# Sliding-window attention with a gated MLP: q and k transposes in PSUM banks of their own, evictions and loads in another order

## The chip, the cores and the metric

One core of a Trainium2 chip. The time is device microseconds of one execution of the program, as a median over runs; lower is better.

## What is computed

```python
# attention, per batch (8) and head (8): 576 positions, head size 64
scores = q @ k.T / sqrt(64)
mask   = (0 <= i - j) & (i - j < 64)          # the last 64 positions
attn   = softmax(where(mask, scores, -1e9))
x      = attn @ v                              # heads side by side: (8, 576, 512)
# gated MLP, per batch
h      = relu(x @ w_in)                        # (576, 1024)
u, v   = h[..., :512], h[..., 512:]
v_n    = (v - mean(v)) / sqrt(var(v) + 1e-6)   # over the last axis
v_s    = einsum('ts,bsd->btd', w_spatial, v_n) + b_spatial[None, :, None]
out    = (u * v_s) @ w_out                     # (8, 576, 512), float32
```

## The kernel before

The kernel works batch by batch. While the MLP of batch a runs, the attention of batch a+1 is worked in between its pieces, and q, k and v of later batches are loaded. Each engine executes its instructions in the order in which the program writes them; that order is written by hand, as strings of two-letter pieces that `run(a, ...)` reads.

The attention of a batch has five steps s: four for the head pairs 0 to 3 over 512 positions, and a fifth for the last 64 positions of all heads. A step goes through these pieces:

- `T` (batches 0 to 3 only): TensorE transposes k and q of the pair into one PSUM tile `tp` (`T_mm`), and `T_out` copies them to `tr` in SBUF, k on VectorE (DVE, L180) and q on ScalarE (ACT, L183). For batches 4 to 7 DVE does this itself, without TensorE, in two halves of two instructions each (`turn`, L147; letters T, or R one batch further ahead).
- `A`: the scores `sc` (`emit_S`), the exponential on ACT and the minimum with a mask on DVE (`E_exp`, `E_mask`), then for the step before it the products with v and the row sums (`emit_P`, tile `oz`), their logarithm and the exponential of its negative on ACT (`ln`, `zi`), and the product `x` on DVE (`N_mul`). The `x` product is written behind the next MLP piece; F writes it at once.

The MLP of a batch goes through V (five row blocks of v: matmul, ReLU on ACT, statistics `st` and `mv` on DVE; p are parts of the matmul and o the eviction; Q is the fifth block, which shares its PSUM tile with the last output block of the batch before and writes that block's store), L (layer norm: two small ACT operations, five DVE operations `vn`, L514), U (five column blocks of u with a ReLU on ACT), W (in batch 0 only, the transposes of w_spatial and their copies), G (the product with w_spatial, and on DVE the product `g` with u) and O (the output blocks, copied on ACT and stored by SP's queue, L476).

PSUM has two banks for `sc`, two for `oz`, and four for everything else, which are handed out in turn (tag "mm"). SP's queue issues the loads of q, k, v and the stores in program order, and waits in that order. POOL casts and shifts the loaded data (`batch_in`, L177). The tiles of loaded data have two buffers, those of cast q and k have one.

The prologue runs the attention of batch 0 pair by pair, with matmuls on zeros (`warm`) in between, and then half of the V matmuls of batch 0 ahead of its P of step 3.

## Time and profile before

| | |
|---|---|
| median of 3 runs | 246.35 us (244.47 to 248.13) |
| profiled execution | 246.02 us, span 244.3 us |
| PE, DVE, ACT, POOL busy, share of the span | 85%, 65%, 64%, 48% |
| prologue, up to the first U matmul of batch 0 (30.06) | 30.06 us |
| batch 0, up to the first transpose for batch 1's stage (63.93) | 33.87 us |
| batch 1, up to batch 2's first V matmul (93.75) | 29.82 us |
| batches 2, 3 (from V to V) | 30.11, 27.21 us |
| batches 4, 5, 6 | 24.25, 24.26, 23.12 us |
| batch 7, to the end | 21.60 us |

The stages are cut by hand at the starts of instructions. A row of a timeline gives the start, the time, the engine, the line of the kernel, the operation and its operands, how many such instructions are put together, and in brackets how long the engine stood idle before it and what ended that. "PE" is TensorE. A share of busy time is an average over stages with different limits, so the table is read by stage.

### The profile page before, as it was taken

The numbers are of one execution on the slowest core, as the hardware profiler recorded it, in microseconds if no ns is written. First come the engines' busy times: TensorE is split into PE (matmuls) and PEld (weight loads), VectorE is DVE, ScalarE is ACT, GpSimd is POOL, SyncE is SP. The second block draws the span as 40 slices with busy tenths as digits, with TensorE's granted clock in tenths as the row PEclk, the third lists the DMA queues.
The fourth block names the chain that finished last, engine by engine and source line by source line (L and its number), as shares of the span: only waits on it lengthen the run. The fifth ranks groups of instructions, "written<-read, shape, count | busy, mean of one in ns | idle before, by whom it ended". The sixth has DMA issues, their size and how long they took to land.

```text
span 244.3 us, 6707 instructions
## 1 busy us (share of the span) xinstructions
PE 207.1 (85%) x2727; PEld 112.1 (46%) x2727; DVE 157.8 (65%) x312; ACT 156.4 (64%) x284; POOL 118.0 (48%) x162
## 2 busy tenths in 40 slices
PE   7577896876976778966999699989998999999993
PEld 2345344553443444534544454545454545554451
DVE  6554379735544753676767677897789778774650
ACT  2365585476476665678578547884788578957713
POOL 3999648999104992227700794992099100000000
PEclk9995999999997999999999799999999999999999
DMA  6999999995009956999999999599960032004105
GB/s 188 300 194 267 217 281 184 275 204 181 4 9 269 262 92 209 196 196 212 200 194 268 244 201 201 180 201 195 180 212 10 3 128 66 6 3 173 24 0 193
DMA packets 77647, 40.43 MB, mean 165 GB/s; under 512 B 44272, under 2 KB 73008, under 8 KB 77616
## 3 DMA queue, kind: packets, MB, share of 16 engines
q1 hardware_dynamic: 75392, 37.76, 70.0%
q0 software_dynamic: 2224, 2.24, 5.4%
q8 instruction: 21, 0.34, 0.7%
q14 instruction: 10, 0.08, 0.2%
HBM read 32.79 MB, written 9.44 MB: 173 GB/s over the span
## 4 chain that ended last, share of the span: by engine, by line
PE 47%; DVE 26%; ACT 20%; issue 5%; POOL 0%; ACTq 0%; POOLq 0%
PE ps L544 11%; PE po L563 11%; PE pv L457 9%; DVE vn L514 6%; ACT e L359 6%; DVE x L429 5%; DVE st L466 4%; DVE tr L180 4%; ACT tr L183 4%; PE oz L394 3%; ACT zi L421 3%; DVE e L375 3%; PE oz L404 2%; ACT vs L464 2%; PE pv L491 2%
## 5 line engine op out<-in xcount | busy, mean ns | idle before, releaser
L177 POOL COPY vs<-vn 64x512 f16<-64x512 f16 (+1 forms) x56 | 44.9, 802 | 3.1
L375 DVE TENSOR_TENSOR e<-e,mask 128x1024 f16<-128x1024 f16 x32 | 27.1, 846 | 28.3 <-ACT e L359 28.3
L177 POOL CAST nk<-fk 128x512 f16<-128x512 f32 (+2 forms) x24 | 20.3, 846 | 51.2 <-DVE tr L147 25.1
L544 PE MATMUL ps<-wspT,vn 128*128 128x512 f16 (+1 forms) x160 | 40.1, 394 | 5.5 <-ACT tr L183 2.3
L429 DVE TENSOR_TENSOR x<-oz,zi 128x512 f16<-128x512 f32 (+1 forms) x40 | 25.3, 633 | 25.7 <-ACT zi L421 25.0
L359 ACT ACTIVATE e<-sc 128x1024 f16<-128x1024 f32 x32 | 32.9, 1028 | 11.1 <-PE sc L317 7.1
L457 PE MATMUL pv<-win,x 128*128 128x512 f16 (+1 forms) x132 | 32.2, 384 | 1.1 <-DVE x L429 1.1
L177 POOL CAST vn<-vf 128x512 f16<-128x512 f32 (+1 forms) x40 | 27.3, 692 | 9.2 <-DMA vf<-in_v_dram 8.5
L466 DVE BATCH_NORM_STATS2 st<-vs 128x6 f32<-128x512 f16 (+1 forms) x40 | 27.0, 675 | 7.3 <-ACT vs L464 6.9
L524 PE MATMUL pu<-x,win 128*128 128x512 f16 x128 | 30.4, 380 | 0.0
L563 PE MATMUL po<-wout,g 128*128 128x512 f16 x128 | 30.2, 379 | 0.0
L464 ACT ACTIVATE vs<-pv 128x512 f16<-128x512 f32 (+1 forms) x40 | 23.0, 596 | 9.0 <-PE pv L457 7.0
L183 ACT COPY tr<-tp 128x512 f16<-128x512 f16 x16 | 9.4, 586 | 29.2 <-DVE tr L180 29.2
L566 ACT COPY ob<-po 128x512 f32<-128x512 f32 x32 | 18.7, 586 | 12.0 <-PE po L563 12.0
L177 POOL CAST nq<-fq 128x512 f16<-128x512 f32 (+2 forms) x27 | 22.3, 825 | 8.3 <-DMA fq<-in_q_dram 8.1
L547 DVE TENSOR_TENSOR g<-ps,ru 128x512 f16<-128x512 f32 x32 | 21.9, 686 | 6.2 <-PE ps L544 6.0
L412 ACT ACTIVATE ln<-oz 128x512 f32<-128x512 f32 (+1 forms) x40 | 22.3, 559 | 5.6 <-PE oz L404 5.6
L544 PEld LDWEIGHTS <-vn 128*128 128x128 f16 (+1 forms) x160 | 14.8, 100 | 23.1 <-issue 5.7
L421 ACT ACTIVATE zi<-ln 128x512 f32<-128x512 f32 (+1 forms) x40 | 23.7, 592 | 0.8
L514 DVE TENSOR_SCALAR vn<-vs,mv,rs 128x512 f16<-128x512 f16 (+1 forms) x40 | 19.8, 560 | 1.2 <-ACT rs L506 1.2
L394 PE MATMUL oz<-e,onesK 128*64 128x512 f16 x64 | 13.4, 410 | 6.8 <-DVE x L429 6.6
L457 PEld LDWEIGHTS <-x 128*128 128x128 f16 (+1 forms) x132 | 12.1, 99 | 15.3 <-DVE x L429 1.6
(81 smaller groups left out, 298.8 us busy)
## 6 DMA issues: line engine op xcount, KB each, us to landing
out_dram<-ob SPq DMA_DIRECT2D x32, 256.0 KB, 3.5
vf<-in_v_dram SPq DMA_DIRECT2D x40, 128.0 KB, 5.1
fk<-in_k_dram SPq DMA_DIRECT2D x32, 144.0 KB, 4.8
fq<-in_q_dram SPq DMA_DIRECT2D x32, 144.0 KB, 5.8
fk<-in_k_dram SPq DMA_DIRECT2D x16, 256.0 KB, 4.9
fq<-in_q_dram SPq DMA_DIRECT2D x16, 256.0 KB, 5.2
vf<-in_v_dram SPq DMA_DIRECT2D x16, 256.0 KB, 6.6
win<-in_moe_w_in_dram POOLq DMA_DIRECT2D x2, 512.0 KB, 8.4
```

The costliest lines, as they stand in the source:

```text
L177: nc.gpsimd.tensor_copy(o, i)
L359: nc.scalar.activation(e2[:, :, :], sc[0][:, :, :], AF.Exp, bias=0.0, scale=0.125)
L375: nc.vector.tensor_tensor(e2[:, :, :], e2[:, :, :], m, ALU.min)
L421: nc.scalar.activation(zinv[:, 0:n], lnz[:, 0:n], AF.Exp, bias=0.0, scale=-1.0)
L429: nc.vector.tensor_tensor(x[:, 0:n], oz[:, 0, 0:n], zinv[:, 0:n], ALU.mult)
L457: nc.tensor.matmul(PV[b, j][0:jn, :], xcol(b, r, j), w_in_sb[:, r, 512:1024], start=(r == 0), stop=(r == 3))
L464: nc.scalar.activation(vs[0:jn, :], pv[0:jn, :], AF.Relu)
L466: nc.vector.bn_stats(st6[0:jn, 0:6], vs[0:jn, :])
L514: nc.vector.tensor_scalar(vn[0:jn, :], vs[0:jn, :], mv[0:jn, j, 0:1], rs[0:jn, j:j + 1], ALU.subtract, ALU.mult)
L524: nc.tensor.matmul(pu[:, :], w_in_sb[:, r, 128 * m:128 * m + 128], X[b, r][:, :], start=(r == 0), stop=(r == 3))
L544: nc.tensor.matmul(ps[:, :], VN[b, kk][0:kn, 128 * m:128 * m + 128], wspT[kk][0:kn, 0:512], start=(kk == 0), stop=(kk == 4))
L563: nc.tensor.matmul(po[:, :], G[b, r][:, 128 * j:128 * j + 128], w_out_sb[:, r, :], start=(r == 0), stop=(r == 3))
```

## The change

The change has these parts:

1. `T_mm` gives k and q a PSUM tile each (two of the four "mm" banks instead of one), and `T_out` copies the fifth step's q on ACT and no longer on DVE.
2. In the prologue `T_out` stands ahead of `N_mul`; the masks are made with fewer, larger copies, and `maskr`, `mv` and `vn4` are filled behind the first `T_out`; there are 3 warming matmuls where 4 were, and 4 more ahead of P of step 3; three quarters of V stand behind that P.
3. For batches 0 and 1 the ReLU of the V blocks 1 and 3 is done by DVE.
4. The strings of batches 0 to 3 are written anew: the attention of the next batch starts earlier (Y is the first transpose of the batch after next), statistics and norm stand behind the evictions of the transposes, and batch 3 has the string of the batches after it.
5. Batch 3's load is issued at the end of batch 0's string, ahead of the store of batch 0's last block, and no longer behind that store in Q of batch 1. The loads of batches 5 to 7 (a+3) move from Q of batch a to the end of batch a's string, ahead of the next store of a last block. Batch 4's load stays at the end of batch 1's string.

```diff
--- before.py
+++ after.py
@@ -213,22 +213,25 @@
                             base=64, channel_multiplier=-1, pattern=[[1, 64]])
     mask = cpool.tile([128, 2, 8, 64], f16, name="mask")
     maskr = cpool.tile([128, 8, 64], f16, name="maskr")
-    for u in range(8):
-        if u % 2 == 1:
-            nc.vector.tensor_copy(mask[:, 0, u, :], keep[:])
-        else:
-            nc.vector.tensor_scalar(mask[:, 0, u, :], keep[:], -1.0, BIG, ALU.mult, ALU.add)
-    nc.vector.memset(mask[64:128, 0, 0, :], 0.0)
+    nc.vector.tensor_scalar(mask[:, 0, 0, :], keep[:], -1.0, BIG, ALU.mult, ALU.add)
+    nc.vector.tensor_copy(mask[:, 0, 1, :], keep[:])
+    nc.vector.tensor_copy(mask[:, 0, 2:4, :], mask[:, 0, 0:2, :])
+    nc.vector.tensor_copy(mask[:, 0, 4:8, :], mask[:, 0, 0:4, :])
     nc.vector.tensor_copy(mask[:, 1, :, :], mask[:, 0, :, :])
-    for u in range(8):
-        nc.vector.tensor_copy(maskr[:, u, :], mask[:, 0, 2, :])
+    for h in (0, 1):
+        nc.vector.memset(mask[64:128, h, 0, :], 0.0)
 
     NSB = 2
     mv_t = [cpool.tile([128, 5, 2], f32, name=f"mv{i}") for i in range(NSB)]
     vn4_t = [cpool.tile([65, 512], f16, name=f"vn4_{i}") for i in range(NSB)]
-    for i in range(NSB):
-        nc.vector.memset(mv_t[i][:], 1.0)
-        nc.vector.memset(vn4_t[i][64:65, :], 1.0)
+
+    def late_consts():
+        nc.vector.tensor_copy(maskr[:, 0, :], mask[:, 0, 2, :])
+        for n in (1, 2, 4):
+            nc.vector.tensor_copy(maskr[:, n:2 * n, :], maskr[:, 0:n, :])
+        for i in range(NSB):
+            nc.vector.memset(mv_t[i][:], 1.0)
+            nc.vector.memset(vn4_t[i][64:65, :], 1.0)
 
     w_in_sb = cpool.tile([128, 4, 1024], f16, name="win")
     w_out_sb = cpool.tile([128, 4, 512], f16, name="wout")
@@ -256,31 +259,28 @@
     TP = {}
 
     def T_mm(b, s):
-        tp = psp.tile([128, 1024], f16, tag="mm", bufs=4, name=f"tp{b}_{s}")
+        tp = [psp.tile([128, 512], f16, tag="mm", bufs=4, name=f"tp{b}_{s}{x}") for x in "kq"]
         TP[b, s] = tp
-        n = 512 if s < 4 else 256
         with nc.named_scope(f"T{b}_{s}"):
             for y, x in enumerate("kq"):
                 w = NH[b, x, s]
                 for t in range(4):
                     if s < 4:
-                        nc.tensor.transpose(tp[:, n * y + 128 * t:n * y + 128 * t + 128],
+                        nc.tensor.transpose(tp[y][:, 128 * t:128 * t + 128],
                                             w[:, 128 * t:128 * t + 128], id16[:, :])
                     else:
-                        nc.tensor.transpose(tp[:, n * y + 64 * t:n * y + 64 * t + 64],
+                        nc.tensor.transpose(tp[y][:, 64 * t:64 * t + 64],
                                             w[0:64, 128 * t:128 * t + 128], id16[0:64, 0:64])
 
     def T_out(b, s):
         tp = TP.pop((b, s))
         o = TR[b][:, :, :].rearrange("p x (a n) -> p x a n", a=4)
-        for y in (0, 1):
+        for y, copy in ((0, dve_copy), (1, act_copy)):
             if s < 4:
-                (act_copy if y == 1 else dve_copy)(
-                    o[:, y, s, 0:512].rearrange("p (n t) -> p n t", t=4),
-                    tp[:, 512 * y:512 * y + 512].rearrange("p (t n) -> p n t", t=4))
+                copy(o[:, y, s, 0:512].rearrange("p (n t) -> p n t", t=4),
+                     tp[y][:, :].rearrange("p (t n) -> p n t", t=4))
             else:
-                nc.vector.tensor_copy(o[:, y, :, 512:576],
-                                      tp[:, 256 * y:256 * y + 256].rearrange("p (a n) -> p a n", a=4))
+                copy(o[:, y, :, 512:576], tp[y][:, 0:256].rearrange("p (a n) -> p a n", a=4))
 
     def emit_T(b, s):
         T_mm(b, s)
@@ -461,7 +461,10 @@
         jn = 128 if j < 4 else 64
         pv = PV.pop((b, j))
         vs = mpool.tile([128, 512], f16, tag=f"vs{j}", bufs=1, name=f"vs{b}_{j}")
-        nc.scalar.activation(vs[0:jn, :], pv[0:jn, :], AF.Relu)
+        if b < 2 and j % 2 == 1:
+            nc.vector.tensor_scalar_max(vs[0:jn, :], pv[0:jn, :], 0.0)
+        else:
+            nc.scalar.activation(vs[0:jn, :], pv[0:jn, :], AF.Relu)
         st6 = mpool.tile([128, 8], f32, tag="st6", bufs=6, name=f"st6{b}_{j}")
         nc.vector.bn_stats(st6[0:jn, 0:6], vs[0:jn, :])
         nc.vector.bn_aggr(mv_t[b % NSB][0:jn, j, :], st6[0:jn, 0:6])
@@ -601,6 +604,8 @@
             if c == "A":
                 if a + 1 < B:
                     att(a + 1, n)
+            elif c == "Y":
+                emit_T(a + 2, n)
             elif c == "T":
                 if a + 1 < NPE:
                     emit_T(a + 1, n)
@@ -622,12 +627,6 @@
             else:
                 if c == "Q":
                     emit_VO4(a)
-                    if a == 1:
-                        load_any(3)
-                        batch_in(3)
-                    elif 1 < a and a + 3 < B:
-                        load_any(a + 3)
-                        batch_in(a + 3)
                 elif c == "L":
                     emit_LN(a)
                 elif c == "W":
@@ -683,9 +682,11 @@
             warm(2)
         if s > 0:
             E_mask(0, s - 1)
+        T_out(0, s)
         if s > 1:
             N_mul(0, s - 2)
-        T_out(0, s)
+        if s == 0:
+            late_consts()
         emit_S(0, s)
         E_exp(0, s)
         if s == 3:
@@ -695,47 +696,48 @@
             emit_N1(0, s - 1)
             N_exp(0, s - 1)
         if s < 3:
-            warm(4)
-    T_out(0, 4)
-    E_mask(0, 3)
-    N_mul(0, 2)
+            warm(3)
     v_in(0, 4)
     load_wsp()
     load_wout()
     load_pairs(2)
     batch_in(1)
 
+    T_out(0, 4)
+    E_mask(0, 3)
+    N_mul(0, 2)
     emit_S(0, 4)
     E_exp(0, 4)
-    run(0, "p0002 p0102 p0202 p0302")
+    warm(4)
     emit_P(0, 3)
     emit_N1(0, 3)
     emit_N2(0, 3)
     E_mask(0, 4)
-    run(0, "p0023 p0123 p0223 p0323 p0034 o0 p0134 o1")
+    run(0, "p0003 p0103 p0203 p0303")
     emit_P(0, 4)
+    run(0, "p0034 p0134 p0234 p0334 o0 o1 o2 o3")
     emit_N1(0, 4)
     emit_N2(0, 4)
-    run(0, "p0234 o2 p0334 o3")
-    run(0, "U0 U1 T0 U2 Q A0 F U3 L W0 W1 W2 W3 W4 U4 T1 G0 A1 G1 G2 T2 G3 A2 G4")
+    run(0, "U0 U1 T0 U2 Q A0 F U3 T1 L A1 U4 W0 W1 W2 W3 W4 G0 G1 T2 A2 G2 G3 G4")
     batch_in(2)
-    run(0, "O0 O1 T3 A3 O2 O3 T4 F A4 F p1002 p1102")
-    run(0, "A5 p1202 p1302 p1023 p1123 p1223 p1323 F")
+    run(0, "O0 T3 A3 O1 O2 T4 F A4 F O3")
+    load_any(3)
+    run(0, "Y0 p1002 p1102 A5 p1202 p1302 p1023 p1123 p1223 p1323 F")
 
     for a in range(1, B):
         if a == 1:
-            run(a, "p0034 o0 p0134 o1 p0234 o2 p0334 o3 T0 U0 T1 U1 A0 Q L T2 U2 U3 A1 U4 G0 T3 A2 "
-                   "G1 G2 A3 T4 G3 G4 A4 O0 O1 A5 O2 O3")
-            load_any(4)
-            batch_in(4)
+            run(a, "A0 p0034 p0134 p0234 p0334 o0 o1 o2 o3 U0 T1 U1 A1 Q T2 F L U2 A2 U3 U4 T3 "
+                   "G0 A3 G1 G2 T4 G3 A4 G4 O0 O1 A5 O2 O3")
         elif a == 2:
-            run(a, "V0 T0 V1 T1 A0 V2 V3 Q T2 A1 F L U0 U1 U2 T3 A2 U3 U4 G0 T4 A3 G1 G2 G3 A4 "
-                   "G4 O0 O1 A5 O2 O3")
-        elif a == 3:
-            run(a, "T0 V0 V1 A0 V2 V3 Q A1 F L T1 U0 U1 U2 U3 A2 U4 G0 A3 G1 G2 G3 A4 G4 R0 O0 O1 "
-                   "A5 O2 R1 O3")
+            run(a, "V0 T0 V1 A0 V2 T1 V3 Q A1 T2 F L U0 U1 U2 A2 T3 U3 U4 G0 A3 T4 G1 G2 G3 A4 "
+                   "G4 R0 O0 O1 A5 O2 R1 O3")
         else:
             run(a, "V0 V1 A0 V2 V3 Q A1 F L U0 U1 U2 A2 U3 U4 G0 A3 G1 G2 G3 A4 G4 R0 O0 O1 A5 O2 R1 O3")
+        if a == 1:
+            batch_in(3)
+        if a + 3 < B:
+            load_any(a + 3)
+            batch_in(a + 3)
     run(B, "Q")
 
 
```

What this does to the order on three engines, at the places in question. In the names, the digits are step or block numbers; `tr`, `e`, `x`, `vn`, `wspT`, `g` are the tiles named above.

First DVE, in batch 0's MLP, from the mask of batch 1's first step to G. Before:

```order
L375 TENSOR_TENSOR e2_1_0_734<-e2_1_0_734,mask_175 128x1024
L514 TENSOR_SCALAR vn0_0_749<-vs0_0_625,mv0_195,rs0_746 128x512
L514 TENSOR_SCALAR vn0_1_751<-vs0_1_632,mv0_195,rs0_746 128x512
L514 TENSOR_SCALAR vn0_2_753<-vs0_2_657,mv0_195,rs0_746 128x512
L514 TENSOR_SCALAR vn0_3_755<-vs0_3_664,mv0_195,rs0_746 128x512
L514 TENSOR_SCALAR vn4_0_197<-vs0_4_711,mv0_195,rs0_746 64x512
L180 COPY wspT3_209<-wps3_779 128x576
L180 COPY wspT4_210<-wps4_786 64x576
L180 COPY tr1_123<-tp1_1_813 128x512
L547 TENSOR_TENSOR g0_0_832<-ps0_0_825,ru0_0_670 128x512
L375 TENSOR_TENSOR e2_1_1_852<-e2_1_1_852,mask_175 128x1024
L547 TENSOR_TENSOR g0_1_884<-ps0_1_877,ru0_1_678 128x512
```

and now:

```order
L375 TENSOR_TENSOR e2_1_0_732<-e2_1_0_732,mask_175 128x1024
L180 COPY tr1_123<-tp1_1k_743 128x512
L517 TENSOR_SCALAR vn0_0_760<-vs0_0_640,mv0_184,rs0_757 128x512
L517 TENSOR_SCALAR vn0_1_762<-vs0_1_645,mv0_184,rs0_757 128x512
L517 TENSOR_SCALAR vn0_2_764<-vs0_2_650,mv0_184,rs0_757 128x512
L517 TENSOR_SCALAR vn0_3_766<-vs0_3_655,mv0_184,rs0_757 128x512
L517 TENSOR_SCALAR vn4_0_186<-vs0_4_709,mv0_184,rs0_757 64x512
L375 TENSOR_TENSOR e2_1_1_787<-e2_1_1_787,mask_175 128x1024
L429 TENSOR_TENSOR x1_0_834<-oz1_0_790,zi1_0_832 128x512
L180 COPY wspT3_194<-wps3_857 128x576
L180 COPY wspT4_195<-wps4_864 64x576
L550 TENSOR_TENSOR g0_0_878<-ps0_0_871,ru0_0_667 128x512
```

The k copy of step 1 has moved ahead of the five norm operations, and the mask of step 1 and the x product of step 0 ahead of the copies of w_spatial, behind which G waits.

Then SP's queue, from the second store of batch 0's output to batch 3's first loads. Before:

```order
L476 DMA out_0_dram<-ob0_1_1030 128x512
L476 DMA out_0_dram<-ob0_2_1094 128x512
L476 DMA out_0_dram<-ob0_3_1107 128x512
L476 DMA out_0_dram<-ob0_4_1315 64x512
L83 DMA fk3_1318<-in_k_dram 128x2x256
L83 DMA fq3_1324<-in_q_dram 128x2x256
L122 DMA vf3_1331<-in_v_dram 128x4x64 x2
```

and now:

```order
L479 DMA out_0_dram<-ob0_1_1086 128x512
L479 DMA out_0_dram<-ob0_2_1099 128x512
L479 DMA out_0_dram<-ob0_3_1168 128x512
L83 DMA fk3_1171<-in_k_dram 128x2x256
L83 DMA fq3_1177<-in_q_dram 128x2x256
L122 DMA vf3_1184<-in_v_dram 128x4x64 x2
L83 DMA fk3_1171<-in_k_dram 128x2x256
```

The store of the last block (64x512), which waits for the next batch's Q, now stands behind all of batch 3's loads.

Last, DVE at batch 4's turns. Before, in the middle of batch 3's string, around its norm:

```order
L514 TENSOR_SCALAR vn3_1_2573<-vs3_1_2379,mv1_196,rs3_2568 128x512
L514 TENSOR_SCALAR vn3_2_2575<-vs3_2_2427,mv1_196,rs3_2568 128x512
L514 TENSOR_SCALAR vn3_3_2577<-vs3_3_2438,mv1_196,rs3_2568 128x512
L514 TENSOR_SCALAR vn4_1_198<-vs3_4_2453,mv1_196,rs3_2568 64x512
L147 STREAM_TRANSPOSE tr4_1768<-nk4_1765 128x9x2x32
L147 STREAM_TRANSPOSE tr4_1768<-nq4_1767 128x9x2x32
L375 TENSOR_TENSOR e2_4_2_2648<-e2_4_2_2648,mask_175 128x1024
L429 TENSOR_TENSOR x4_1_2695<-oz4_1_2651,zi4_1_2693 128x512
```

and now at the end of batch 2's string:

```order
L559 TENSOR_TENSOR g2_4_2269<-ps2_4_2247,ru2_4_2089 128x256
L429 TENSOR_TENSOR x3_3_2273<-oz3_3_2225,zi3_3_2271 128x512
L147 STREAM_TRANSPOSE tr4_1775<-nk4_1772 128x9x2x32
L147 STREAM_TRANSPOSE tr4_1775<-nq4_1774 128x9x2x32
L429 TENSOR_TENSOR x3_4_2320<-oz3_4_2295,zi3_4_2318 128x256
L147 STREAM_TRANSPOSE tr4_1775<-nk4_1772 128x9x2x32
```

The second half of batch 4's turn (tr4) stood behind batch 3's norm and ahead of the mask of batch 4's third step; now the first half stands between the x products of batch 3's last two steps, and the second half follows.

## Rows read from the trace of the kernel before

**Rows 1.** Stages: us, busy PE, PEld, DVE, ACT, POOL (instructions), clock, DMA share, GB/s.

```profile
0.00:30.06 30.06, 21.42 (x249) 11.46 (x249) 15.07 (x46) 13.81 (x20) 23.04 (x41) 0.89 1.10 234
30.06:63.93 33.87, 27.09 (x337) 15.53 (x335) 20.92 (x40) 21.70 (x41) 26.11 (x41) 1.00 0.92 206
63.93:93.75 29.82, 22.52 (x298) 13.13 (x298) 17.30 (x35) 18.31 (x34) 15.58 (x24) 0.94 0.59 143
93.75:123.86 30.11, 24.53 (x315) 13.93 (x314) 18.52 (x36) 19.83 (x37) 13.09 (x14) 1.00 1.10 204
123.86:151.07 27.21, 24.58 (x356) 13.05 (x355) 19.76 (x36) 18.48 (x35) 13.08 (x14) 0.94 1.18 222
151.07:175.32 24.25, 23.19 (x355) 12.34 (x354) 20.36 (x34) 18.09 (x35) 13.56 (x14) 1.00 0.95 192
...
199.58:222.70 23.12, 22.77 (x355) 12.21 (x354) 16.11 (x32) 18.17 (x35) 0.00 (x0) 1.00 0.15 54
```

**Rows 2.** Timeline of the prologue: start us, us, engine, line, operation.

```profile
1.26 4.20 PE L197 MATMUL warm<-scratch 128*128 128x512 f16 x12 [1.26 <-DVE scratch L192]
...
6.62 0.69 DVE L180 COPY tr<-tp 128x512 f16<-128x512 f16 x1 [0.71 <-PE tp L267]
...
7.35 0.59 ACT L183 COPY tr<-tp 128x512 f16<-128x512 f16 x1 [5.26 <-DVE tr L180]
...
7.98 0.42 PE L301 MATMUL sc<-tr 64*64 64x128 f16 x16 [0.97 <-ACT tr L183]
...
21.21 0.64 PE L301 MATMUL sc<-tr 64*64 64x128 f16 x16 [1.40 <-ACT tr L183]
```

**Rows 3.** Timeline of PE, batch 0's first G matmuls.

```profile
41.24 1.24 PE L544 MATMUL ps<-wspT,vn 128*128 128x512 f16 x5 [1.57 <-DVE wspT L180]
```

**Rows 4.** Timeline of PE, batch 1's first G matmuls.

```profile
75.90 2.29 PE L544 MATMUL ps<-wspT,vn 128*128 128x512 f16 x5 [2.26 <-ACT tr L183]
```

**Rows 5.** Timeline of PE, P matmuls in batch 2's stage.

```profile
108.59 0.41 PE L394 MATMUL oz<-e,onesK 128*64 128x512 f16 x2 [1.76 <-DVE x L429]
...
114.56 0.41 PE L394 MATMUL oz<-e,onesK 128*64 128x512 f16 x2 [1.80 <-DVE x L429]
```

**Rows 6.** Timeline of batch 3's stage: norm on DVE, scores on PE.

```profile
133.51 1.69 DVE L514 TENSOR_SCALAR vn<-vs,mv,rs 128x512 f16<-128x512 f16 x5
...
136.60 0.66 PE L317 MATMUL sc<-tr 32*64 32x128 f16 x32 [2.42 <-DVE tr L147]
```

**Rows 7.** Timeline of SP's queue: a store, and batch 4's first loads.

```profile
53.05 19.36 SPq L476 DMA_DIRECT2D out_dram<-ob  x5
...
94.99 1.93 SPq L117 DMA_DIRECT2D fk<-in_k_dram  x4
```

**Rows 8.** Timeline of POOL: casts and copies of batch 4.

```profile
110.80 1.15 POOL L177 CAST nq<-fq 128x1152 f16<-128x1152 f32 x1 [3.41 <-DMA fq<-in_q_dram]
...
117.34 2.14 POOL L177 COPY vs<-vn 64x1024 f16<-64x1024 f16 x2
```

**Rows 9.** Timeline of batch 4's stage: P and G on PE, norm on DVE.

```profile
156.72 0.41 PE L394 MATMUL oz<-e,onesK 128*64 128x512 f16 x2
...
164.65 0.39 PE L544 MATMUL ps<-wspT,vn 65*128 65x512 f16 x1 [0.71 <-DVE vn L514]
...
160.58 4.02 DVE L514 TENSOR_SCALAR vn<-vs,mv,rs 128x512 f16<-128x512 f16 x5
```

**Rows 10.** Page, part 5: groups of instructions, mean in ns.

```profile
L375 DVE TENSOR_TENSOR e<-e,mask 128x1024 f16<-128x1024 f16 x32 | 27.1, 846 | 28.3 <-ACT e L359 28.3
...
L429 DVE TENSOR_TENSOR x<-oz,zi 128x512 f16<-128x512 f32 (+1 forms) x40 | 25.3, 633 | 25.7 <-ACT zi L421 25.0
L359 ACT ACTIVATE e<-sc 128x1024 f16<-128x1024 f32 x32 | 32.9, 1028 | 11.1 <-PE sc L317 7.1
...
L412 ACT ACTIVATE ln<-oz 128x512 f32<-128x512 f32 (+1 forms) x40 | 22.3, 559 | 5.6 <-PE oz L404 5.6
...
L421 ACT ACTIVATE zi<-ln 128x512 f32<-128x512 f32 (+1 forms) x40 | 23.7, 592 | 0.8
```

## Prediction

> **What bounds the kernel now.** I read the busy time of every engine by stage first, with the stages cut where the first V matmul (or, for batch 1, the first transpose) of a batch starts [rows 1]. The stage of batch 4 takes 24.25 us and PE works 23.19 of them: PE is the bound there. The stage of batch 6 takes 23.12. The stages of batches 0 to 3 take 33.87, 29.82, 30.11 and 27.21, and PE works 27.09, 22.52, 24.53 and 24.58. So 3 to 7 us of each early stage are waits, and the 30.06 us ahead of them are a chain with warming matmuls in it. Whatever the change brings has to come from the first 151 us. From there on PE has nothing to give but the last microsecond between 24.25 and 23.12.
>
> The waits themselves, in order of time. In the prologue, the ACT copy of the transposed q starts at 7.35, when the DVE copy of k that began at 6.62 is over, though both transposes were in the bank by then; the scores start at 7.98 [rows 2]. In batch 0's stage G begins at 41.24 after 1.57 us of waiting for a DVE copy that stands behind the layer norm [rows 3]. In batch 1's stage G waits 2.26 us and then takes 2.29 us for five matmuls that take 1.24 elsewhere; the granted clock of that stage is 0.94, and the engine had just stood still [rows 1, 4]. In batch 2's stage the P matmuls of two steps wait 1.76 and 1.80 us for the DVE product x of the step before [rows 5]. In batch 3's stage PE waits 2.42 us for DVE's second turn of batch 4, ahead of its third score step [rows 6], and the granted clock of that stage is 0.94 as well [rows 1].
>
> **The parts, one by one.** *Batch 3 (the surest term).* Its string becomes that of batches 4 to 7: the turns of batch 4 stand at the end of batch 2's string, and the turn on which PE waited is gone from the middle. Work and order are then those of the stage that takes 24.25 us, so 27.21 - 24.25 = 2.96 us go: the wait of 2.42 and the slow matmuls behind it. For nothing, if the data to be turned is there: batch 4's load leaves at the same place as before (end of batch 1's string), and its last q cast ended 17.0 us after the first issue (110.80 + 1.15 - 94.99) [rows 7, 8]; the turns now stand behind the G matmuls of a stage of 27 us, more than 20 us after that issue. The O matmuls and the next batch's first V matmuls cover them; without that cover PE would wait as it did before, 2.42 us.
>
> *Batches 4 and 5.* The loads of batches 5 to 7 move from near the head of a stage to its end, about 17 us later, and with them POOL's casts and copies. Before, these lay beside the layer norm: its five DVE operations take 4.02 us at 160.58 with POOL at work and 1.69 at 133.51, where POOL waits; PE stands 0.71 us for the last of them [rows 6, 9]. Afterwards POOL is paced by the arriving transfers, one 1.15 us cast at a time [rows 8]. Batch 6 shows the stage with POOL idle, 23.12 [rows 1]; I take half of 24.25 - 23.12, about 0.55 us, for each of batches 3, 4 and 5: 1.65 us. Bounds: 0 and 3.4.
> The Trainium skill (SBUF — State Buffer, Who interferes with whom) says that DVE and GpSimd share a port pair as an exclusive lock, so one side waits for the other's whole instruction. The 4.02 against 1.69 agrees; by the rule one cast in the stretch would leave 1.69 + 1.15 = 2.84 us, again half of the difference, and the sum stays.
>
> *Batch 2.* The statistics of each V tile are now behind the evictions of k and q, the k and q copies run at once, and the copies of T4 are split between the engines. Each of five pairs loses 0.7 us of latency (7.35 - 6.62) [rows 2], where the step waits for it. The two waits of P, 1.76 + 1.80 us [rows 5], had the x product queued behind the mask, which waited for the exponentials, which waited for this serial pair: of 3.56 I count 2.0 as gone, and 0.5 for the two transposes that no longer stand ahead of the first V's statistics. Two turns at the end of the string are hidden behind the O matmuls, as in batch 4. 2.5 us, so 27.6 remain. Bounds: 0 (then P waits for something else) and 30.11 - 24.53 = 5.6.
>
> *The prologue.* The first scores come 1.1 us earlier: 0.7 from the pair, and some 0.4 because DVE reaches the cast of k before it has made the small masks and constants; the 12 warming matmuls (1.26 + 4.20 = 5.46) forbid more [rows 2]. The constants come back behind the first eviction, so the second step gains no more than the first. From then on the step's period was (21.21 - 7.98)/3 = 4.41 us [rows 2]; with the copies together and the x product behind them it is the ACT chain: scores 0.42, exponential 1.03, ln 0.56, its exponential 0.59, q copy 0.59 and 0.2 of hand-over, 3.4 us [rows 2, 10]. Two such steps: 2.0 more, 3.1 in all. P of step 3 then meets POOL's shift copies of V, whose chain is not changed, and three quarters of V now stand behind it instead of half; I let 2.5 us through to the end of V.
>
> *Batches 0 and 1: what is paid.* Two ReLUs of each batch go to DVE, 0.69 us apiece by the copy of the same shape [rows 2]: 1.4 us on the engine that sets the statistics, and now two of the four banks that the transposes need are held until DVE gets there, while U waits behind them on PE. In batch 0 a k copy, a mask and an x product (0.69 + 0.85 + 0.63 [rows 2, 10]) go ahead of the copies on which G waits: 2.2 us. So G of batch 0 starts at 41.24 - 2.5 + 1.4 + 2.2 = 42.3, later than before. What is bought is the scores and P of the second pair (0.42 and about 0.8 of PE) ahead of G instead of behind it, and later the first transposes and scores of batch 2 before batch 1's stage begins. In batch 1 G also comes later than 75.90, behind one more attention step, its relus and a k copy. The pair copies win 0.7 us a step here too, but only where the chain goes through them. I put the balance of both stages at -1.3 us, which leaves 1.2 of the prologue's 2.5. Bounds: -5 and +3.
>
> *The early load of batch 3.* SP stood 19.36 us from 53.05 in the store that waits for batch 1's Q, and the load queued behind it [rows 7]. Now it leaves some 16 us earlier. Its data was not waited for (batch 3's transposes run from 94 on), so I count nothing; its cost is below.
>
> **Sum.** 2.96 + 1.65 + 2.5 + 1.2 = 8.3 us. The profiled execution took 246.02 us (span 244.3), so 237.7 by that; the median of the runs is 0.33 above it, so I say 238.0.
>
> **Rivals.** *DVE and the banks become the early bound.* For it: PE has only four such banks, T takes two, and DVE's ReLUs stand between its statistics; PE standing there can also lose its clock, as in batch 1 before. Then batches 0 and 1 cost 2 us more each: 242. Against it: DVE is busy only 20.92 of 33.87 and 17.30 of 29.82 there [rows 1].
> *The early stages fill up.* Attention of batch 2 begins before batch 1's norm, so batch 1 may come within 3 us of its PE time of 22.52 [rows 1]: 29.82 - 25.5 = 4.3 more, 233.7. For it: 7 us of waits are there. Against: the norm chain itself is untouched.
> *POOL's casts of batch 3 now meet the norm of batch 1.* It ran before that load had left (72.4, the end of SP's wait [rows 7]; G of batch 1 started at 75.90 [rows 4]). With POOL beside it the norm takes 4.02 and not 1.69 [rows 6, 9], and G comes 2.3 us later: 240.3. Against: these casts wait for batch 2's transposes, which stand well apart in the new string. It is the rule of the Trainium skill named above, turned against the change.
> *The loads come too late (slower).* A load of batch a+3 now starts about 1.2 us into stage a+1 (94.99 - 93.75), and POOL's last copy of V that the first P needs ends 24.5 us later (117.34 + 2.14 - 94.99) [rows 7, 8], at 25.7; that P stands 5.65 us into stage a+2 (156.72 - 151.07) [rows 1, 9], at 24.25 + 5.65 = 29.9. The slack is 4.2 us; each microsecond beyond it is paid in batches 4, 5 and 6. A chain 7 us longer eats the whole gain (3 x 2.8 = 8.4), and one 9 us longer gives 238 + 3 x 4.8 = 252.4. For it: the DMA share is 1.10 and 1.18 in the stages of batches 2 and 3 [rows 1]. Against: the measured chain of batch 4 had the same neighbours.
> *The copies don't run together,* since PE still delivers q after k and ACT is late anyway: the 2.0 of the prologue's steps and most of batch 2's 2.5 go, 242.
>
> **How the numbers follow.** Forecast 0.45, early stages filled 0.18, casts against the norm 0.10, DVE and banks 0.14, copies not together 0.05, loads late 0.08. The first three are faster by over 2% (below 241.4), about 0.70 with the tails; the next two lie within 2% (about what a measurement of this kernel can tell from no change), 0.22; the last is slower, 0.08. The range of 8 in 10 goes from the filled case to the bank case: 233.0 to 243.5; the forecast's own range is 235 to 241.
>
> **What would show it.** ACT's q copy should start within 0.3 us of DVE's k copy in all steps. The stage of batch 3 should take 23.1 to 24.3 us, with no wait of PE for a turn; batches 4 and 5 under 24.25 with a norm below 3 us; batch 2 26 to 29. S of step 3 of the prologue should start near 18. G of batch 0 should start later than its scores of pair 2. Wrong would be: PE waiting for POOL or a turn after 120 us, or V of batch 2 starting later than 93.75.

## The result, and the profile after

The changed kernel takes 233.77 us (median of 4 runs, 232.19 to 234.47); the ratio to the kernel before is 0.948, interval 0.938 to 0.959. The forecast was 238.0 us, range 233.0 to 243.5, faster by over 2% with a chance of 0.70. The side and the range hold, the value is 4.2 us too high, and the experiments show that the parts of the sum were mis-sized in both directions.

The profiled execution took 233.42 us with a span of 231.7, 12.6 less than before. Stages of the changed kernel, cut at the first U matmul and then at the first V matmul of batches 2 to 7; columns as in [rows 1]:

```profile
0.00:30.33 30.33, 22.80 (x249) 11.88 (x250) 17.58 (x38) 13.89 (x21) 20.86 (x40) 0.89 1.10 232
30.33:91.54 61.21, 49.79 (x634) 27.28 (x634) 40.90 (x76) 39.28 (x72) 41.62 (x67) 0.97 0.81 182
91.54:117.43 25.89, 24.36 (x316) 13.27 (x314) 20.11 (x37) 20.02 (x38) 12.10 (x13) 1.00 0.91 184
117.43:140.56 23.13, 22.78 (x356) 12.23 (x355) 18.09 (x34) 18.17 (x35) 9.86 (x12) 1.00 1.00 202
140.56:163.68 23.12, 22.76 (x355) 12.21 (x354) 18.81 (x34) 18.17 (x35) 12.95 (x15) 1.00 1.03 211
163.68:186.80 23.12, 22.77 (x355) 12.21 (x354) 18.50 (x34) 18.17 (x35) 12.88 (x16) 1.00 1.03 206
186.80:209.92 23.12, 22.77 (x355) 12.20 (x354) 16.12 (x32) 18.17 (x35) 3.14 (x4) 1.00 0.16 54
209.92:231.70 21.78, 18.00 (x117) 8.26 (x115) 9.45 (x21) 10.13 (x20) 0.00 (x0) 0.98 0.26 88
```

Against [rows 1]: the prologue is no shorter (30.33 after 30.06). Batches 0 and 1 together take 61.21 after 33.87 + 29.82 = 63.69, batch 2 takes 25.89 after 30.11, and batches 3 to 5 now equal batch 6. PE has 11.4 us to spare in batches 0 and 1 and about 0.35 in each of batches 3 to 6.

The waits of ACT for a transposed tile show what went. The waits page of the kernel before (engine, line, waited for: us in total, times, longest), for the q copy and for PE's scores behind it:

```profile
ACT tr L183 <- DVE tr L180: 29.2, 15, 5.3
PE sc L301 <- ACT tr L183: 11.3, 10, 1.8
```

and every such row in the changed kernel:

```profile
ACT tr L183 <- PE tp_0q L269: 4.5, 1, 4.5
ACT tr L183 <- PE tp_1q L269: 3.8, 2, 3.3
ACT tr L183 <- PE tp_2q L269: 3.7, 2, 2.7
ACT tr L183 <- PE tp_4q L272: 1.0, 1, 1.0
PE sc L301 <- ACT tr L183: 1.6, 3, 0.7
PE sc L309 <- ACT tr L183: 1.6, 1, 1.6
```

ACT no longer waits for DVE before a q copy, only for the transposes, at the program's start and where it is early anyway. PE's scores wait 3.2 us for q copies, where they waited 11.3.

### The profile page after: what moved, and what is told of

Same layout as the page of the kernel before. It is cut to its first block, busy times and chain, and to the rows that moved or that the text cites. A ratio compares the mean times of both kernels' runs of the same rounds, so it can differ in the third digit from the quotient of the medians.

```text
span 231.7 us, 6707 instructions
## 1 busy us (share of the span) xinstructions
PE 206.0 (89%) x2728; PEld 109.5 (47%) x2728; DVE 159.5 (69%) x305; ACT 156.0 (67%) x284; POOL 113.4 (49%) x162
## 4 chain that ended last, share of the span: by engine, by line
PE 46%; ACT 16%; DVE 12%; DMA 12%; POOL 5%; issue 4%; SPq 3%; POOLq 0%; ACTq 0%
PE ps L547 10%; PE po L566 8%; PE pv L457 6%; DMA fq<-in_q_dram 5%; DMA fk<-in_k_dram 4%; PE warm L197 4%; ACT e L359 3%; PE oz L394 3%; ACT zi L421 3%; SPq L117 3%; ACT ru L529 3%; DMA vf<-in_v_dram 3%; DVE st L469 3%; POOL vs L177 3%; DVE x L429 3%
## 5 line engine op out<-in xcount | busy, mean ns | idle before, releaser
L177 POOL COPY vs<-vn 64x512 f16<-64x512 f16 (+1 forms) x56 | 42.5, 760 | 3.1
L177 POOL CAST nk<-fk 128x512 f16<-128x512 f32 (+2 forms) x24 | 19.7, 819 | 40.0 <-DMA fk<-in_k_dram 28.0
L547 PE MATMUL ps<-wspT,vn 128*128 128x512 f16 (+1 forms) x160 | 37.7, 379 | 0.5 <-ACT tr L183 0.4
L375 DVE TENSOR_TENSOR e<-e,mask 128x1024 f16<-128x1024 f16 x32 | 25.9, 811 | 17.2 <-ACT e L359 17.2
L177 POOL CAST vn<-vf 128x512 f16<-128x512 f32 (+1 forms) x40 | 25.6, 647 | 11.0 <-DMA vf<-in_v_dram 10.1
L467 ACT ACTIVATE vs<-pv 128x512 f16<-128x512 f32 (+1 forms) x36 | 21.2, 596 | 12.8 <-PE pv L457 9.3
L529 ACT ACTIVATE ru<-pu 128x512 f32<-128x512 f32 x32 | 17.7, 599 | 1.9 <-PE pu L527 1.8
L527 PEld LDWEIGHTS <-win 128*128 128x128 f16 x128 | 11.4, 97 | 13.8 <-issue 2.3
L517 DVE TENSOR_SCALAR vn<-vs,mv,rs 128x512 f16<-128x512 f16 (+1 forms) x40 | 16.9, 487 | 0.7 <-ACT rs L509 0.6
```

The lines of the kernel that those rows point to most:

```text
L177: nc.gpsimd.tensor_copy(o, i)
L375: nc.vector.tensor_tensor(e2[:, :, :], e2[:, :, :], m, ALU.min)
L527: nc.tensor.matmul(pu[:, :], w_in_sb[:, r, 128 * m:128 * m + 128], X[b, r][:, :], start=(r == 0), stop=(r == 3))
L529: nc.scalar.activation(ru[:, :], pu[:, :], AF.Relu)
L547: nc.tensor.matmul(ps[:, :], VN[b, kk][0:kn, 128 * m:128 * m + 128], wspT[kk][0:kn, 0:512], start=(kk == 0), stop=(kk == 4))
```

## The experiments

All stages in one table, in us, each from the kernel's profiled execution, cut at the first U matmul and at the first V matmul of a batch, to 0.2 us (some records are missing). The cuts from batch 4 on lie 0.16 to 0.17 us earlier here than in [rows 1]. Each ratio is to runs of the kernel before that were taken beside it (medians 245.76 to 247.34).

| kernel | median | ratio to before | to first U | batches 0+1 | batch 2 | 3 | 4 | 5 |
|---|---|---|---|---|---|---|---|---|
| before | 246.35 | | 30.06 | 63.69 | 30.11 | 27.05 | 24.25 | 24.25 |
| changed | 233.77 | 0.948 [0.938, 0.959] | 30.33 | 61.21 | 25.89 | 23.13 | 23.12 | 23.12 |
| changed, one tile for the pair | 247.37 | 1.005 [1.000, 1.009] | 33.56 | 68.56 | 31.01 | 23.12 | 23.12 | 23.12 |
| before + tiles | 232.67 | 0.948 [0.942, 0.954] | 30.00 | 55.43 | 25.25 | 25.93 | 24.06 | 24.23 |
| changed, loads of 5 to 7 early | 236.34 | 0.961 [0.955, 0.968] | 31.40 | 60.32 | 25.88 | 23.12 | 23.12 | 23.94 |
| before + late loads | 244.36 | 0.995 [0.992, 0.999] | 28.87 | 63.38 | 30.15 | 27.01 | 23.12 | 23.12 |
| before + batch 3's string | 244.64 | 0.993 [0.989, 0.996] | 30.10 | 65.21 | 30.14 | 24.25 | 24.26 | 24.25 |
| changed, batch 3's load back | 233.29 | 0.946 [0.940, 0.952] | 30.27 | 61.21 | 25.90 | 23.12 | 23.12 | 23.12 |
| changed, constants later | 230.63 | 0.936 [0.931, 0.941] | 28.38 | 61.27 | 25.89 | 23.13 | 23.12 | 23.13 |
| changed, batch 2's old string | 232.26 | 0.946 [0.940, 0.951] | 29.40 | 61.34 | 25.26 | 23.12 | 23.12 | 23.11 |
| before + tiles, loads, batch 3 | 227.23 | 0.924 [0.919, 0.929] | 30.27 | 55.56 | 25.26 | 23.12 | 23.12 | 23.12 |
| changed, old strings 0 and 1 | 232.40 | 0.942 [0.935, 0.948] | 31.63 | 58.95 | 25.89 | 23.13 | 23.12 | 23.12 |
| the gains alone | 225.42 | 0.917 [0.913, 0.921] | 28.01 | 56.21 | 25.25 | 23.12 | 23.12 | 23.12 |
| changed, ReLUs on ACT | 230.14 | 0.931 [0.923, 0.939] | 30.88 | 57.84 | 25.89 | 23.12 | 23.11 | 23.12 |

The column of the first U is the noisy one: the six kernels with the changed prologue show 29.40 to 31.63 there. The other columns repeat to 0.1 us where the same code runs, but for batches 0 and 1 (60.32 to 61.34 over five kernels with one code there, save for the place of batch 3's load, and 63.38 to 65.21 over three with the code of before). Of the kernels with a single part undone, only that with one tile has a ratio whose interval is clear of the changed kernel's; the others are read from their stages.

**The tiles, taken away and alone.** One tile again, in the changed kernel:

```diff
-        tp = [psp.tile([128, 512], f16, tag="mm", bufs=4, name=f"tp{b}_{s}{x}") for x in "kq"]
+        both = psp.tile([128, 1024], f16, tag="mm", bufs=4, name=f"tp{b}_{s}")
+        tp = [both[:, 0:512], both[:, 512:1024]]
```

> The changed kernel with one edit undone: k and q of a step are transposed into one PSUM tile again, so that the q copy on ACT waits for the k copy on DVE; all else as changed. Theory A (the separate tiles give each step that the chain goes through about 0.7 us): the prologue's four steps, batch 0, batch 1 and batch 2 lose 0.4 to 0.7 us a step where PE waits for the copies: some 3 to 5 us, 237 to 239 in all, batches 3 to 7 unchanged to 0.1 us. Theory B (the rival of the banks: two of four banks held by a transposed pair is what the early stages wait for, and ACT is late anyway): a single tile gives a bank back, and the time stays at 233 to 234.5 or falls.

Measured: 247.37 us, no faster than before. The whole gain is gone, 13.6 us, nearly three times the most that theory A allowed. (Its profiled execution was 1.7 us above its median, at a granted clock of 0.948, so its early stages may be up to that much too long in the table.) Its waits page:

```profile
ACT tr L183 <- DVE tr L180: 34.2, 19, 5.8
PE sc L302 <- ACT tr L183: 19.8, 15, 3.7
```

The reverse, the kernel before with the new `T_mm` and `T_out` and nothing else:

> The kernel before with one edit alone: k and q of a step in PSUM tiles of their own, and the fifth step's q copied on ACT; order and loads as before. Theory A (the pair was the early chain): the first scores 0.7 us earlier, some 0.7 us for each of the steps on which PE waited, 3 to 4 us in all, 242 to 243. Theory B (the order of evictions against statistics and norm was the chain, and the pair is hidden behind it): within 1 us of the kernel before, 245.5 to 247. Theory C (four banks are too few when a pair takes two, and the old order puts them where U and V want one): slower by 1 us or more.

Measured: 232.67 us, as fast as the whole change, and again far beyond theory A (3 to 4 us); theories B and C fall. The new `T_out` also copies the fifth step's q on ACT; the kernel with one tile above keeps that and loses the whole gain, so the gain is not from there. Batches 0 and 1 get 8.3 us shorter, batch 2 4.9, batch 3 1.1. The reason stands in batch 2's stage. ACT in the kernel before:

```profile
94.81 0.60 ACT L464 ACTIVATE vs<-pv 128x512 f16<-128x512 f32 x1 [0.28 <-PE pv L457]
96.96 0.59 ACT L183 COPY tr<-tp 128x512 f16<-128x512 f16 x1 [1.55 <-DVE tr L180]
97.45 0.60 ACT L464 ACTIVATE vs<-pv 128x512 f16<-128x512 f32 x1
99.60 0.59 ACT L183 COPY tr<-tp 128x512 f16<-128x512 f16 x1 [1.55 <-DVE tr L180]
...
104.84 0.59 ACT L183 COPY tr<-tp 128x512 f16<-128x512 f16 x1 [1.69 <-DVE tr L180]
```

and DVE in the same stage:

```profile
95.44 0.69 DVE L466 BATCH_NORM_STATS2 st<-vs 128x6 f32<-128x512 f16 x1 [1.00 <-ACT vs L464]
96.17 0.18 DVE L467 BATCH_NORM_AGGREGATE mv<-st 128x2 f32<-128x6 f32 x1
96.27 0.66 DVE L180 COPY tr<-tp 128x512 f16<-128x512 f16 x1
```

The q copy waits for the k copy; the k copy stands behind the statistics on DVE; the statistics wait for ACT's ReLU, which runs just before the q copy. So the two engines run in turn: ReLU (ACT), statistics and k copy (DVE), q copy (ACT), and ACT stands 1.55 us each time, not the 0.7 us of the k copy. In the kernel with tiles alone, ACT at the same place:

```profile
86.49 0.60 ACT L461 ACTIVATE vs<-pv 128x512 f16<-128x512 f32 x1 [0.28 <-PE pv L454]
86.98 0.58 ACT L183 COPY tr<-tp_0q 128x512 f16<-128x512 f16 x1
87.80 0.60 ACT L461 ACTIVATE vs<-pv 128x512 f16<-128x512 f32 x1 [0.24 <-PE pv L454]
88.29 0.58 ACT L183 COPY tr<-tp_1q 128x512 f16<-128x512 f16 x1
```

The q copy follows its ReLU at once, and runs ahead of the k copy (87.95 on DVE). The statistics still stand ahead of the k copy there, and it costs little: what PE stands idle in the stage (its length less PE's busy time) falls from 5.58 us (30.11 - 24.53) to 1.01 (25.25 - 24.24). The Trainium skill (PSUM — Partial Sum Buffer, PSUM bank collisions raise a hardware error) says that two engines must be kept apart, reads too, by semaphores per bank and group of 32 partitions. The wait agrees: it stands before the q copy 15 times with one tile (29.2 us), and never with two.

Batch 3's stage gains by another way. PE waits there for the turn as long as before, 2.43 us after 2.42 [rows 6], but the granted clock of the 2.9 us from the end of that wait is 1.00, the upper level, and was 0.62 before. With the tiles alone:

```profile
123.41 0.66 PE L314 MATMUL sc<-tr 32*64 32x128 f16 x32 [2.43 <-DVE tr L147]
...
125.07 1.25 PE L541 MATMUL ps<-wspT,vn 128*128 128x512 f16 x5
```

and the same G matmuls in the kernel before:

```profile
138.94 2.12 PE L544 MATMUL ps<-wspT,vn 128*128 128x512 f16 x5
```

So one wait of this length was followed by the upper level and one by the lower; what made the difference is not shown.

**The loads.** Back near the head of a stage, in the changed kernel:

```diff
                 if c == "Q":
                     emit_VO4(a)
+                    if 1 < a and a + 3 < B:
+                        load_any(a + 3)
+                        batch_in(a + 3)
...
-        if a + 3 < B:
+        if a == 1:
             load_any(a + 3)
             batch_in(a + 3)
```

> The changed kernel with the loads of batches 5 to 7 (and their casts on POOL) back near the head of a stage, in Q of batch a; batch 3's load stays where the change put it. Theory A (POOL's casts beside the layer norm cost the last microsecond of the stages of batches 3 to 5): their stages go from 23.13, 23.12, 23.13 to about 24.25 each, the five norm operations from 1.69 to 2.5 to about 4.0, 3.4 us in all: 237. Theory B (the stages gained that by their strings or by the order of the output stores): they stay at 23.1 and the time at 233 to 234.5.

Theory A expected three stages of about 24.25 and a norm of about 4.0 in each; the profile shows only that of batch 5 longer, 23.94. In batch 3's stage the norm ran between two casts of POOL, and took 1.69 us (126.98). The five norm operations in the changed kernel, batch 4's stage:

```profile
149.93 2.52 DVE L517 TENSOR_SCALAR vn<-vs,mv,rs 128x512 f16<-128x512 f16 x5
```

and with the loads early, stages of batches 4 and 5:

```profile
150.09 2.69 DVE L517 TENSOR_SCALAR vn<-vs,mv,rs 128x512 f16<-128x512 f16 x5
173.21 4.00 DVE L517 TENSOR_SCALAR vn<-vs,mv,rs 128x512 f16<-128x512 f16 x5
```

A norm of 2.5 to 2.7 us costs the stage nothing, one of 4.00 costs 0.8. The median is 2.6 above the changed kernel's, but the intervals of the two ratios overlap, and the profiled execution was the fastest of the four; what the others lost is not in a trace. The reverse, in the kernel before:

> The kernel before with one edit alone: the loads of batches 5 to 7 at the end of batch a's string instead of in Q of batch a. Theory A (casts beside the norm): the stages of batches 4 and 5 go from 24.25 and 24.26 to about 23.1, batch 3's stage from 27.21 to 26 to 27, together 2.3 to 3.4 us, 243 to 244.5. Batch 2's stage, whose turns stand in batch 3's string, does not change. Theory B (the loads come too late for P or for the turns): PE waits for a V copy or a turn after 120 us and the time rises above 247.

Batches 4 and 5 go to 23.12 each, 1.13 us less, as theory A said; batch 3's stage does not move while its turn is in the middle (27.01). In time 0.5%, and at the end of its interval 0.9% or 2.1 us, so the time confirms the 2.3 us of the two stages only in part.

Batch 3's load alone, back behind the store:

```diff
                 if c == "Q":
                     emit_VO4(a)
+                    if a == 1:
+                        load_any(3)
...
-    load_any(3)
```

> The changed kernel with batch 3's load back in Q of batch 1, behind the store that waits for it. Theory A (the data was not waited for): no change beyond 0.3 us, 233.3 to 234.2, perhaps with batch 1's norm at 1.69 instead of 1.92. Theory B (with batch 3's transposes now earlier in the string, the load must be early too): PE waits for a cast of batch 3 in batch 2's stage, which grows from 25.89 by 1 to 4 us: 235 to 238.

No change in any stage: theory A, and the nothing that the prediction counted.

**Batch 3's string alone,** in the kernel before:

```diff
-                   "G4 O0 O1 A5 O2 O3")
-        elif a == 3:
-            run(a, "T0 V0 V1 A0 V2 V3 Q A1 F L T1 U0 U1 U2 U3 A2 U4 G0 A3 G1 G2 G3 A4 G4 R0 O0 O1 "
-                   "A5 O2 R1 O3")
+                   "G4 R0 O0 O1 A5 O2 R1 O3")
```

> The kernel before with one edit alone: batch 4's turns on DVE stand at the end of batch 2's string and batch 3 has the string of the batches behind it. Theory A (PE's wait for the second turn, 2.42 us, and the slow matmuls behind it are all that sets batch 3 apart): batch 3's stage goes from 27.21 to 24.25, batch 2's stays near 30.1, 3 us in all, 243.5. Theory B (the turns only move into batch 2's tail and are paid there): batch 2's stage grows by 1 to 2.5 us and the time stays within 1 us of the kernel before.

Batch 3's stage takes 24.25, the value of the prediction to the hundredth, and batch 2's stays at 30.14. By time 0.7%; batches 0 and 1 of the profiled execution took 1.5 us longer with unchanged code, so theory A rests on the stages.

**The constants of the prologue.**

```diff
-        if s == 0:
-            late_consts()
...
     N_mul(0, 2)
+    late_consts()
     emit_S(0, 4)
```

> The changed kernel with one move: the small constants on DVE (three copies of the mask, four fills), which now stand behind the first eviction of the prologue and ahead of the k cast of step 1, go behind the x product of step 2, where DVE stands idle for 2.80 us. Theory A (these 3.3 us on DVE are why the prologue gained nothing: T of step 1 starts at 11.43, 3.00 us after PE was ready): the second scores come at about 10 instead of 13.04, and the first U 1 to 3 us earlier than 30.33: 231 to 233 in all. Theory B (the prologue's end is set by POOL's shift copies of V or by the loads): S of steps 1 and 2 earlier, but the first U still at 30 to 30.4, and the time unchanged.

Measured 230.63 us, first U at 28.38: theory A. That first U lies below the spread of the six kernels above, as does that of the other kernel with this move (28.01, the gains alone). DVE in the changed kernel:

```profile
6.40 0.69 DVE L180 COPY tr<-tp_0k 128x512 f16<-128x512 f16 x1 [2.15 <-PE tp_0k L269]
...
7.22 1.94 DVE L231 COPY maskr<-maskr 128x64 f16<-128x64 f16 x3
...
10.57 0.80 DVE L180 CAST nk<-fk 128x512 f16<-128x512 f32 x1
```

and PE in it:

```profile
11.43 0.40 PE L269 MATMUL tp_1k<-id,nk 128*128 128x128 f16 x4 [3.00 <-DVE nk L180]
...
13.04 0.64 PE L301 MATMUL sc<-tr 64*64 64x128 f16 x16 [0.55 <-DVE tr L180]
...
21.21 0.42 PE L301 MATMUL sc<-tr 64*64 64x128 f16 x16 [0.67 <-ACT tr L183]
```

The cast of step 1's k stands behind the constants, PE waits 3.00 us for it, and the granted clock is then 0.50, the lower level of 1.2 GHz, from 13.04 to 17.70 (0.64 for scores that take 0.42). The kernel before had the same scores earlier:

```profile
11.88 0.42 PE L301 MATMUL sc<-tr 64*64 64x128 f16 x16 [1.63 <-ACT tr L183]
```

With the constants later, the fourth scores start at 17.95 instead of 21.21:

```profile
17.95 0.42 PE L301 MATMUL sc<-tr 64*64 64x128 f16 x16 [0.96 <-ACT tr L183]
```

**Batch 2's old string,** with separate tiles and the turns at its end:

```diff
-            run(a, "V0 T0 V1 A0 V2 T1 V3 Q A1 T2 F L U0 U1 U2 A2 T3 U3 U4 G0 A3 T4 G1 G2 G3 A4 "
+            run(a, "V0 T0 V1 T1 A0 V2 V3 Q T2 A1 F L U0 U1 U2 T3 A2 U3 U4 G0 T4 A3 G1 G2 G3 A4 "
```

> The changed kernel with the first part of batch 2's string as before (T1 ahead of A0, T2 ahead of A1, T3 ahead of A2, T4 ahead of A3), and the two turns at its end. Theory A (the order ahead of A is what batch 2 gained by): its stage goes from 25.89 back by 2 us or more, 28 to 30, and P waits for x again, 1 to 2 us at two places: 236 to 237.5. Theory B (separate tiles and the later loads did it): the stage stays at 25.9 to 26.5, and the time at 233.5 to 234.5.

The stage gets shorter, 25.26: theory B and more. The new order in batch 2 costs 0.6 us.

**The parts that gain, put together.** First the kernel before with tiles, late loads and batch 3's string:

> The kernel before with three parts of the change: tiles of their own for k and q, the loads of batches 5 to 7 at the end of a string, and batch 3 with the string of the batches behind it (batch 4's turns at the end of batch 2's). Prologue and the strings of batches 0 and 1 as before, and the first part of batch 2's. Theory A (the parts add, and the new early strings cost time now that the copies run together): batch 2's first V at 85.4 as with the tiles alone, then 25.25, four stages of 23.12 and 21.78: a span of 224.9, 226.6 in all. Theory B (the early strings of the change are needed once the loads and turns come later): PE waits for a cast or a turn in batches 2 to 4, 228 or more.

227.23 us, stages as theory A gave them. So the rest of the change costs 6.5 us. Then the changed kernel with the strings of batches 0 and 1 as before:

> The changed kernel with the strings of batches 0 and 1 (and the place of batch 3's load in Q of batch 1) as before; the two ReLUs a batch on DVE, the prologue and all else stay. Theory A (the new strings cost the 5.8 us by which batches 0 and 1 are longer than with the tiles alone): from the first U to batch 2's first V 55.5 instead of 61.2 us, 228 in all. Theory B (the ReLUs on DVE cost it): 60 to 61 us, 233 to 234.

58.95 us for batches 0 and 1: between the theories. The strings cost 2.3 us, and 3.4 are left. Then with all ReLUs on ACT, batch 2's old string and the constants later:

> The changed kernel with the strings of batches 0 and 1 and the first part of batch 2's as before, all ReLUs on ACT, and the small constants of the prologue moved to where DVE stands idle. Theory A (all gains add): first U at 28.4, then 55.4, 25.25, four times 23.12 and 21.78: a span of 223.3, 225.0 in all. Theory B (an earlier prologue is given back in batch 0, where POOL's casts of batch 1 set the first transposes): as with tiles, loads and turns alone, 226.6.

225.42 us, theory A (225.0): 8.4 us faster than the changed kernel. Last the ReLUs alone, back on ACT in the changed kernel:

```diff
-        if b < 2 and j % 2 == 1:
+        if False:
```

> The changed kernel with one edit undone: the ReLUs of V blocks 1 and 3 of batches 0 and 1 on ACT again. Theory A (the ReLUs on DVE, ahead of statistics on the engine that all wait for, cost what the old strings did not give back: 58.95 us from the first U to batch 2's first V with the old strings and these ReLUs, 56.2 with neither): 61.2 goes to 58 to 58.5, 230.5 to 231 in all. Theory B (in the new strings the copies of q and the exponentials have filled ACT there, and the ReLUs were rightly moved off it): 61.2 or longer, 233.5 or more.

57.84 us: theory A, 3.4 us. DVE in the changed kernel, batch 1:

```profile
65.81 0.66 DVE L465 TENSOR_SCALAR vs<-pv 128x512 f16<-128x512 f32 x1
...
68.13 0.66 DVE L465 TENSOR_SCALAR vs<-pv 128x512 f16<-128x512 f32 x1
...
69.65 0.66 DVE L180 COPY tr<-tp_1k 128x512 f16<-128x512 f16 x1
```

and PE:

```profile
70.36 0.61 PE L301 MATMUL sc<-tr 64*64 64x128 f16 x16 [2.52 <-DVE tr L180]
...
72.19 0.63 PE L494 MATMUL pv<-win,x 128*64 128x512 f16 x1
```

With the ReLUs on ACT, PE at the same two places:

```profile
67.95 0.42 PE L301 MATMUL sc<-tr 64*64 64x128 f16 x16 [1.53 <-DVE tr L180]
...
69.01 0.38 PE L494 MATMUL pv<-win,x 128*64 128x512 f16 x1
```

The two ReLUs delay the k copy behind them by 2 x 0.66, PE's wait grows from 1.53 to 2.52 us. The stretch behind the wait, in the changed kernel (columns as in [rows 1]),

```profile
70.36:73.60 3.24, 3.24 (x42) 1.59 (x42) 0.72 (x1) 1.59 (x2) 1.79 (x4) 0.51 1.17 257
```

and with the ReLUs on ACT:

```profile
67.95:70.20 2.25, 2.25 (x50) 1.46 (x51) 0.72 (x1) 1.77 (x3) 2.12 (x5) 1.00 1.09 290
```

After 2.52 us of standing the clock is at its lower level (0.51, 0.63 us for a matmul of 0.38), after 1.53 at its upper one. The wait of 2.43 us shown above was followed by the upper level, so the length of the wait alone does not decide it. The 1.3 us on DVE in each of two batches become 3.4 in all: 1.5 in batch 0 and 1.9 in batch 1, cut at batch 1's first V matmul (59.58 and 58.62). The rows above are of batch 1. In batch 0 the x product stands behind the two ReLUs on DVE, and PE waits for it in the changed kernel,

```profile
35.42 1.05 PE L457 MATMUL pv<-win,x 128*64 128x512 f16 x4 [1.49 <-DVE x L429]
```

and not with the ReLUs on ACT:

```profile
34.53 1.05 PE L457 MATMUL pv<-win,x 128*64 128x512 f16 x4
```

## Why the prediction was right, and where it was not

| part | predicted | measured | by the experiments |
|---|---|---|---|
| prologue, batches 0 and 1 | -1.2 | -2.2 | tiles -8.3; strings +1.6 to +2.3; ReLUs +2.7 to +3.4; prologue +0.3 |
| batch 2 | -2.5 | -4.2 | tiles -4.9; new order +0.6 |
| batch 3 | -3.5 | -3.9 | its string -2.8; a norm clear of POOL's work -1.1, with the loads early too |
| batches 4 and 5 | -1.1 | -2.3 | late loads -1.1 each in the kernel before; 0 and -0.8 in the changed kernel |
| sum | -8.3 | -12.6 | |

The parts were measured in different kernels and need not add up; batches 0 and 1 alone spread by 1.0 us and more. That the sum came within the range is in part luck: the tiles were worth 13 us, far more than the pair was given in all terms together, and four other parts gave back 8.4 us, where it had counted 3.6 (1.4 + 2.2).

*The failed step is the price of the pair.* "Each of five pairs loses 0.7 us of latency (7.35 - 6.62)" priced the wait by the duration of the k copy, read in the prologue, where DVE was free (and batch 2 has four such pairs, not five: the fifth step's copies were both on DVE). Where DVE has a queue, the wait is as long as that queue: 1.38 to 1.69 us a step in batch 2, 0.59 to 2.61 where it waited in batches 0 and 1, 29.2 us over 15 steps, 23.9 over 14 without the first one. This row was in the trace before the change, and the prediction did not use it. Of the 3.56 us that P waited for x in batch 2 it counted 2.0 as gone; with the tiles alone none of it is left. It also gave part of the gain of batch 2 to the new order, which in fact cost 0.6. The rival that the copies do not run together was priced at 242 for the same reason; one tile gives 247.4.

*The prologue.* The step that failed is "the constants come back behind the first eviction, so the second step gains no more than the first": they cost the second step 1.2 us (13.04 after 11.88), and what the steps behind it had gained went with it (the fourth scores start at 21.21 in both kernels). The arithmetic of the steps was good: the fourth scores were to start near 18, and do at 17.95 once the constants are out of the way.

*Batches 0 and 1.* The directions were right, ReLUs on DVE and G later as the price (G of batch 0 started at 43.28; 42.3 was predicted), a shorter pair as the gain. Both were far too small: 8.3 of gain by the tiles against 5 to 5.6 of loss by strings and ReLUs, where the prediction had a balance of 1.3. The rival of DVE and the banks describes this loss; it took effect, and was outweighed.

*The rival with the right time.* The early stages filling up was given 233.7, within 0.1 of the result, but not for its reason: batch 1 did not come within 3 us of PE's time (31.96 us from its first V matmul to batch 2's, PE busy for 26.05), and batches 0 and 1 together keep 11.4 us of waits. The agreement is chance.

*The other rivals.* The casts of batch 3 met batch 1's norm only in part: 1.92 us at 76.81, not 4.02. The loads did not come too late: after 120 us PE waits for x alone, four times, 0.35 to 0.36 us.

*Batch 3's string* was right, 24.25 to the hundredth. *The loads* were right in kind and half too small: of 1.13 us the prediction took half, by the norm that remains (2.52 us, where 2.84 was worked out). But a norm of that length costs PE nothing: the step from the norm to the stage was wrong, and there is slack of at least 1.0 us (2.69 against 1.69, with the stage at 23.12). Nor does the changed kernel need the late loads as the kernel before did: with the loads early again, batches 3 and 4 keep their 23.12, and batch 5 loses 0.8. The rule of the Trainium skill (SBUF — State Buffer, Who interferes with whom), that one side waits for the other's whole instruction, gave the 2.84; the trace has one cast beside that norm (150.03) and 2.52, so the rule came out 0.3 us too long.

*What was to show it.* The q copy was to start within 0.3 us of the k copy in all steps. It started 0.22 to 0.43 us after it in three prologue steps, and up to 2.6 us ahead of it later, where DVE had a queue:

```profile
67.02 0.59 ACT L183 COPY tr<-tp_1q 128x512 f16<-128x512 f16 x1 [0.47 <-PE tp_1q L269]
```

with the k copy at 69.65. So the two copies do not run together there either; what went is the wait of one for the other. Batch 2's V starts at 91.54, ahead of 93.75; batch 2's 25.89 is just below its range of 26 to 29.

## What to carry to other kernels

A wait between two engines can last as long as what stands in the releaser's queue, not just the duration of the instruction that releases; read its total from the waits page, as a bound and not as the gain (here 29.2 us of waits on ACT, and 13 us of time). Two engines that copied out of one PSUM tile were coupled by that here, and as each also waited for the other elsewhere, they ran in turn; a tile each takes a few lines and was worth 13 us. Test the parts of a bundled change one by one: the tiles alone gave as much as the whole change, batch 3's string and the late loads gave 5.4 us more (232.67 to 227.23), and four other parts took back 8.4 (233.77 to 225.42).

## What the runs showed that was not expected

Three small copies on DVE of `maskr` took 1.94 us while POOL was busy beside them (7.22 in the changed kernel), and 0.67 us where POOL was idle:

```profile
21.43 0.67 DVE L231 COPY maskr<-maskr 128x64 f16<-128x64 f16 x3
```

That row is from the kernel with the constants later. The first U of one prologue lay anywhere from 29.40 to 31.63 us, a spread larger than many of the effects that were looked for.
